# A gated scan and a top-1 mixture of experts on one Trainium2 core: the first pages picked on TensorE, loads in paced pieces, and a new order of the early work

## The chip, the core and the metric

The kernel runs on one core of one Trainium2 chip. A core has a matrix engine (TensorE, PE in the profile), a vector engine (VectorE, DVE), a scalar engine with function tables (ScalarE, ACT), a general engine (GpSimd, POOL) and a synchronisation engine that here only issues transfers (SyncE, SP). Each engine takes its instructions in the order in which the program wrote them and stands still until the semaphores of the next one are there. Transfers run on DMA engines that all queues share. The metric is the device time of one execution in microseconds (us).

## The reference

The inputs are x, r_gate and i_gate (4 sequences x 5056 steps x 256 channels, float32), a parameter per channel, and a top-1 mixture of 8 experts. The core of it:

```python
a_base = 1 / (1 + exp(-a_param))
log_a = 8 * sigmoid(r_gate) * log(clip(a_base, 1e-6, 1 - 1e-6))
a_t = exp(log_a)
x_gated = sqrt(max(1 - a_t * a_t, 1e-6)) * sigmoid(i_gate) * x
for t in range(S):                 # a scan along the steps
    h = a_t[:, t] * h + x_gated[:, t]
    y[:, t] = h
# 20224 tokens of 256 channels
logits = y @ w_gate + modality_bias[modality_id]
e_idx = argmax(logits)             # one expert a token
gate_w = softmax(logits)[e_idx]
out = gate_w * (relu(y @ w1[e_idx]) @ w2[e_idx])     # 256 -> 1024 -> 256
```

With these inputs two experts ("hot") hold nearly all tokens.

## The kernel before

**Runs and pages.** The 5056 steps are cut into runs (CHUNKS: four of 128 steps, 17 of 256, one of 128, one of 64). A run goes through: loads of a, g, x (L503, SP); tanh of both gates (L550, L535), exp (L556), square (L560) and square root (L562) on ACT; two products, the scan and a size on DVE (L541, L567, L584, L719); a scale out of that size by small matmuls (L595, L606, L608); the split of the scan's result into a high float16 part (L763, ACT) and a low one (L775, DVE); logits on PE (L789), their transpose and the routing on DVE (L845 to L913), ranks within an expert by three matmuls (L883 to L886). The routing's end is `di`, the slot of each token in a table of rows in DRAM, and `b`, how many tokens the hot experts hold by now. The split parts are turned into token rows by transposing DMAs (L814), and POOL scatters the rows to DRAM by their slots (L936).

The mixture of experts works on pages of 256 tokens of one expert (128 in the first pair). DVE chooses a pair of pages, one for each hot expert (`sel`, L1040), by a bound on what the routed runs surely hold: `choose_pages` wants the tokens of the routed runs, less `2 * behind(tokens)`, to reach those already chosen plus a pair. SP reads `sel` into a register, loads the page transposed (`X`, L1169) and its indices and gates (`mt`, L1170). PE multiplies by w1 (`ph`, L1248), ACT and DVE evacuate to a high and a low half of `H` (L1189, L1191), PE multiplies by w2 (`po`, L1290), ACT scales (`ot`, L1200) and POOL scatters to the output (L1204).

**Weights.** The four matrices of the two hot experts (w0 to w3; w2 is the first matrix of the second hot expert) are loaded (L417), measured (L340, L347) and split into a high half (HI: ACT L394 or DVE L397) and a low half (LO: "P" for PE, two passes of L382 and one of L383 with an evacuation by ACT L385; "D" for DVE, L377).

**What sets the order.** Nothing is scheduled on the chip. While the program is written, threads (Python generators) ask for an engine, with an assumed duration and a condition; `run()` takes the thread that can start first, and among those that could start within a small window after it (WINDOW, or URGENT for the early runs) the one with the lowest rank. The rank of a run's threads is a base plus C_STEP times its number. The order in which threads are taken is the order of each engine's instructions. START says in which order runs and weights ("w") are loaded at first.

```python
near = [th for th in threads if th.req[0] == eng and th.start <= first.start + th.window]
th = min(near, key=lambda th: (th.prio[eng != "PE"], th.start))
```

Of the kernel before, what the change touches and what calls it, by code (L numbers as in the profile page):

```python
# [17 lines left out]
P = 128  # L18
# [11 lines left out]
CHUNKS = [(128*k, 128) for k in range(4)] + [(512 + 256 * k, 256) for k in range(17)] + [(4864, 128), (4992, 64)]  # L30
# [6 lines left out]
WINDOW = 0.1  # L37
# [42 lines left out]
def kernel(  # L80
# [74 lines left out]
    nc.vector.tensor_scalar_add(ch, ch, 1.0)  # L155
    nc.vector.reciprocal(ch, ch)
    nc.vector.tensor_scalar(out=ch, in0=ch, scalar1=1e-6, scalar2=1.0 - 1e-6, op0=ALU.max, op1=ALU.min)

    def decay():

        yield "ACT", 0.2, seen(("tanh", 0, "a"), ("tanh", 0, "g")), None, "L"
        nc.scalar.activation(ch, ch, AF.Ln)
        table[0] = "E"
        yield "DVE", 0.1, None
        nc.vector.tensor_scalar_mul(ch, ch, 4.0)
        mark["ch"] = plan["end"] + 0.2
# [254 lines left out]
    def hot_weights(m):  # L421
# [65 lines left out]
    def load_chunk(c):  # L487
# [10 lines left out]
        for i, (name, src) in enumerate((("a", rs), ("g", gs), ("x", xs))):  # L498
            tag = "H" if c == 0 and name != "g" else name
            yield "DMA", 2.9 * z, room(tag), -9.0  # L500
            tickets[c, name] = tag, take(tag)
            t = (pm if tag == "H" else pa).tile([P, cols], F32, name=f"{name}{c}", tag=tag, bufs=BUFS[tag])
            LOADS.dma_start(t, src[:, base : base + cols])  # L503
            got.append(t)
            mark["load", c, name] = plan["end"]
# [262 lines left out]
    def low_parts(c, yg, ys, sc):  # L768
# [30 lines left out]
    def rows_part(c, j):  # L799
# [6 lines left out]
        for s in range(2):  # L806
            for h in range(2):
                yield "DMA", 0.24 * k, allof(room("rt"), high, before or high) if s == h == 0 else first if h == 0 else None, -9.0, 1.18
                if s == h == 0:
# [26 lines left out]
        mark["put", c, j] = plan["end"] + 3.0  # L836

    def route_chunk(c):
# [63 lines left out]
        with nc.allow_low_precision(reason="one whole number and zeros"):  # L902
            nc.vector.tensor_reduce(out=di, in_=ce(dt), axis=AX.X, op=ALU.add)
# [491 lines left out]
```

## Time and profile before

| what | value |
|---|---|
| median of 3 runs | 972.79 us (971.25 to 974.68) |
| the profiled execution, its own time | 970.82 us |
| its span in the profile | 969.0 us |
| mean granted clock of TensorE | 0.984 |
| busy: PE, DVE, ACT, POOL | 913.2, 667.2, 581.9, 433.4 us |
| first matmul of a page | 48.16 us |
| start of the fifth pair of pages (pair 4) | 155.02 us |

The span is cut by the profile's views in several ways: busy time of every engine in chosen stretches, a timeline of each engine in which runs of like instructions make one row (start, length, engine, line, operation, names, shapes, and in brackets the idle time before it with what ended it), and groups by line and shape. "Granted clock" is TensorE's clock as the throttle allowed it, 1.00 being full speed. Pairs of pages are counted from 0; a run's number counts from 0 too.

### The profile page before, as it was taken

To read this page: it belongs to the slowest core of one execution; us is meant where nothing else is said; L and a number is where in the kernel's file an instruction comes from. 1 tells how busy PE (TensorE), PEld (TensorE's weight loads), DVE (VectorE), ACT (ScalarE), POOL (GpSimd) and SP (SyncE) were. 2 spreads that over 40 slices of the span, in tenths; PEclk is the share of its full clock that TensorE was granted. 3 is DMA by queue.
4 is the path that set the end of the run, shared out by engine and by line. 5 is a ranking of instruction groups with operands and counts; after the bars stand their busy time and mean duration, and the time that the engine had idled before them with its cause. 6 is when DMAs were issued, how large, how long until landed. Compare 5 with 4: busy or idle time off the path is not lost. (4 is left out here: it accounts for less than half of the span.)

```text
span 969.0 us, 22431 instructions
## 1 busy us (share of the span) xinstructions
PE 913.2 (94%) x8516; PEld 789.8 (82%) x8516; DVE 667.2 (69%) x1654; ACT 581.9 (60%) x822; POOL 433.4 (45%) x539
## 2 busy tenths in 40 slices
PE   2969896999999999999999999999999999999996
PEld 2457785878888788878888888888989888888886
DVE  6887987999998989989988899743623332223321
ACT  7896766868678767688687795533333333333332
POOL 5433542663557565666655566453441212112112
PEclk9989997999999999999999999999999999999999
DMA  9766776897978889888999976635422112112110
GB/s 321 193 201 208 211 231 137 224 261 213 242 180 224 235 235 226 205 202 210 220 239 263 244 162 130 125 105 147 100 78 58 45 52 59 46 51 61 45 40 18
DMA packets 221735, 156.11 MB, mean 161 GB/s; under 512 B 198129, under 2 KB 201330, under 8 KB 215090
## 3 DMA queue, kind: packets, MB, share of 16 engines
q1 hardware_dynamic: 205296, 110.61, 48.6%
q0 software_dynamic: 16176, 43.98, 13.2%
q8 instruction: 68, 1.11, 0.5%
q14 instruction: 49, 0.40, 0.2%
q10 hardware_dynamic: 146, 0.00, 0.0%
HBM read 68.76 MB, written 44.35 MB: 117 GB/s over the span
## 5 line engine op out<-in xcount | busy, mean ns | idle before, releaser
L1248 PE MATMUL ph<-X,hw 128*128 128x256 f16 (+1 forms) x3936 | 478.4, 273 | 10.9 <-DMA X<-rows 10.9
L1290 PE MATMUL po<-hw,H 128*128 128x256 f16 x3840 | 470.9, 273 | 0.4 <-DVE H L1191 0.4
L1248 PEld LDWEIGHTS <-hw 128*128 128x128 f16 x3936 | 379.1, 99 | 59.8 <-issue 7.5
L1290 PEld LDWEIGHTS <-H 128*128 128x128 f16 x3864 | 374.6, 98 | 46.3 <-issue 1.7
L1191 DVE SCALAR_TENSOR_TENSOR H<-ph,H 128x512 f16<-128x512 f32 (+1 forms) x332 | 220.5, 668 | 240.4 <-ACT H L1189 239.6
L1189 ACT ACTIVATE H<-ph 128x512 f16<-128x512 f32 (+1 forms) x332 | 191.5, 580 | 268.7 <-PE ph L1248 266.6
L1204 POOL DMA_INDIRECT out_dram<-ot,mt x161 | 178.1, 1106 | 285.7 <-ACT ot L1200 237.7
L936 POOL DMA_INDIRECT rows<-rt,di x158 | 186.8, 1182 | 210.8 <-PE po L1290 56.7
L1200 ACT ACTIVATE ot<-po,gt 128x256 f32<-128x256 f32 x161 | 75.9, 472 | 76.8 <-PE po L1290 74.7
L584 DVE TENSOR_TENSOR_SCAN g<-a,g 128x512 f32<-128x512 f32 (+1 forms) x78 | 94.5, 1225 | 0.8
L775 DVE SCALAR_TENSOR_TENSOR a<-g,scy,a 128x512 f16<-128x512 f32 (+2 forms) x92 | 58.9, 677 | 2.9 <-ACT a L763 2.7
L763 ACT ACTIVATE a<-g,scy 128x512 f16<-128x512 f32 (+2 forms) x92 | 55.7, 654 | 0.6 <-DVE scy L615 0.6
L567 DVE SCALAR_TENSOR_TENSOR g<-x,g 128x1024 f32<-128x1024 f32 (+1 forms) x40 | 48.0, 1199 | 9.5 <-ACT x L562 9.4
L556 ACT ACTIVATE a<-a,ch 128x1024 f32<-128x1024 f32 (+2 forms) x46 | 50.7, 1115 | 0.1
L541 DVE SCALAR_TENSOR_TENSOR g<-g,x 128x1024 f32<-128x1024 f32 (+1 forms) x40 | 48.6, 1218 | 0.0
L550 ACT ACTIVATE a<-a 128x2048 f32<-128x2048 f32 (+2 forms) x23 | 38.3, 1667 | 14.7 <-DMA a<-in_r_gate_dram 14.6
L719 DVE TENSOR_REDUCE top<-x 128x4 f32<-128x2048 f32 (+2 forms) x23 | 45.4, 1974 | 2.3 <-DMA x<-in_x_dram 2.2
L562 ACT ACTIVATE x<-x,quarter 128x2048 f32<-128x2048 f32 (+2 forms) x23 | 40.5, 1761 | 0.3
L560 ACT ACTIVATE x<-a 128x2048 f32<-128x2048 f32 (+2 forms) x23 | 38.3, 1666 | 2.8 <-DVE g L541 2.5
L535 ACT ACTIVATE g<-g 128x2048 f32<-128x2048 f32 (+2 forms) x23 | 38.3, 1664 | 0.0
L562 ACT ACT_TABLE_LOAD x22 | 28.2, 1283 | 0.5
L936 POOL DMA_INDIRECT rows<-nt,ni x16 | 16.0, 997 | 19.8 <-PE po L1290 10.3
(195 smaller groups left out, 460.2 us busy)
## 6 DMA issues: line engine op xcount, KB each, us to landing
a<-in_r_gate_dram SPq DMA_DIRECT2D x17, 1024.0 KB
g<-in_i_gate_dram SPq DMA_DIRECT2D x17, 1024.0 KB
x<-in_x_dram SPq DMA_DIRECT2D x17, 1024.0 KB
wr<-in_moe_w_dram SPq DMA_DIRECT2D x4, 1024.0 KB
out_dram<-ot,mt POOLq DMA_INDIRECT x161
a<-in_r_gate_dram SPq DMA_DIRECT2D x5, 512.0 KB
g<-in_i_gate_dram SPq DMA_DIRECT2D x5, 512.0 KB
x<-in_x_dram SPq DMA_DIRECT2D x5, 512.0 KB
```

Of the source, the lines that this page charges most:

```text
L556: nc.scalar.activation(sl, sl, AF.Exp, scale=ch[:, h : h + 1], bias=ch[:, h : h + 1])
L562: nc.scalar.activation(s, s, AF.Sqrt, scale=-0.25, bias=quarter)
L584: nc.vector.tensor_tensor_scan(out=gi, data0=ai, data1=gi, initial=0.0, op0=ALU.mult, op1=ALU.add)
L763: nc.scalar.activation(ys[:, 0, :, g], yg[:, :, g, :].rearrange("p h (k b) -> p h k b", b=Q), AF.Copy, scale=sc[:, g : g + 1])
L775: nc.vector.scalar_tensor_tensor(out=ys[:, 1, :, g], in0=yg[:, :, g, :].rearrange("p h (k b) -> p h k b", b=Q), scalar=sc[:, g : g + 1], i ...
L936: ins = nc.gpsimd.indirect_dma_start(out=rows[:, :], out_offset=bass.IndirectOffsetOnAxis(ap=idx, axis=0), in_=src, in_offset=None, bounds ...
L1189: nc.scalar.activation(t.H[:, 0, hs, :], ph[:, :, 0:st], AF.Relu)
L1191: nc.vector.scalar_tensor_tensor(out=t.H[:, 1, hs, :], in0=ph[:, :, 0:st], scalar=0.0, in1=t.H[:, 0, hs, :], op0=ALU.max, op1=ALU.subtract,)
L1200: nc.scalar.activation(t.ot[:, a, :], po, AF.Copy, scale=t.gt[:, a : a + 1])
L1204: ins = nc.gpsimd.indirect_dma_start(out=out[:, :], out_offset=bass.IndirectOffsetOnAxis(ap=t.mt[:, a, 0:1], axis=0), in_=t.ot[:, a, :], i ...
L1248: ins = nc.tensor.matmul(ph[:, v, 0:st], lhsT, rhs, start=(m == 0), stop=(m == len(mm) - 1))
L1290: ins = nc.tensor.matmul(po, lhsT, rhs, start=(f == 0 and m == 0), stop=(f == NF - 1 and m == len(mm) - 1))
```

## The change

**Runs.** The first run has 96 steps instead of 128 and the last 96 instead of 64; all runs between start 32 steps earlier. **Decay.** The parameter's log (add, reciprocal, clip, Ln, times 4) is issued ahead of the first run's tanh; cpar is alone on ACT's queue, the modality bias goes to SP's. **Loads.** Run 1 is loaded ahead of the first weights (START). A load is cut into pieces of at most 128 steps (512 KB), and from run 2 on each piece waits until the piece two before it has landed. **First pages.** The first pair of pages, 128 tokens for each hot expert, isn't loaded from DRAM: DVE compares the slots of run 0 with the slots of the two pages (one-hot matrices, `pick`), and PE multiplies the token rows of run 0 by them, which gives `Xfirst` already transposed; ACT and DVE copy it out. Its `mt` is loaded as before. **Weights.** The low half of w2 is made on DVE instead of PE; of the high halves of w2 one moves from DVE to ACT. **Order.** The windows shrink, the rank of each of a run's threads gets a table (RANK), and assumed durations change. The gates of a page and the modality's bias of a run are threads of their own.

```diff
-CHUNKS = [(128*k, 128) for k in range(4)] + [(512 + 256 * k, 256) for k in range(17)] + [(4864, 128), (4992, 64)]
+CHUNKS = (
+    [(0, 96)] + [(96 + 128 * k, 128) for k in range(3)] + [(480 + 256 * k, 256) for k in range(17)]
+    + [(4832, 128), (4960, 96)]
+)
-WINDOW = 0.1
+WINDOW = 0.0
-HI = ["A", "D", "AD", "D", "A", "D"]
-LO = "PPPPDD"
-START = "0 w 1 w w w 2"
+HI = ["A", "AD", "AD", "D", "A", "D"]
+LO = "PPDPDD"
+START = "0 1 w w w w 2"
+PACED = 2
-EARLY = 8
-URGENT = 0.3
+EARLY = 7
+URGENT = 0.03
+RANK = {
+    "load": [2.5, 3.1, 0.5, 0.0, 0.0, -0.5, -2.2, 0.0, 1.4],
...
+def place(kind, c):
+    return BASE[kind] + C_STEP * c + (RANK[kind][c] if c < len(RANK[kind]) else 0.0)
...
+    nc.vector.tensor_scalar_add(ch, ch, 1.0)
+    nc.vector.reciprocal(ch, ch)
+    nc.vector.tensor_scalar(out=ch, in0=ch, scalar1=1e-6, scalar2=1.0 - 1e-6, op0=ALU.max, op1=ALU.min)
+    nc.scalar.activation(ch, ch, AF.Ln)
...
-    def decay():
-        yield "ACT", 0.2, seen(("tanh", 0, "a"), ("tanh", 0, "g")), None, "L"
-        nc.scalar.activation(ch, ch, AF.Ln)
...
+        n = max(1, T // P)
+        for name, src in (("a", rs), ("g", gs), ("x", xs)):
...
+            for i in range(n):
...
+                ins = LOADS.dma_start(t[:, i * w : (i + 1) * w], src[:, base + i * w : base + (i + 1) * w])
+                if c >= PACED:
+                    tc.add_manual_dep(
+                        ins.ins, pace[-2], mybir.DependencyInfo(mybir.DependencyClass.Sync, mybir.DependencyReason.DATA)
+                    )
+                pace.append(ins.ins.name)
...
+    def first_pages():
...
+        nc.tensor.matmul(pb[:, 0:HOT], onesf[0:1], u, start=True, stop=True)
...
+            nc.vector.tensor_scalar(out=slot[:, r], in0=along, scalar1=base[:, r : r + 1], scalar2=None, op0=ALU.add)
...
+            nc.vector.tensor_scalar(out=oh, in0=slot, scalar1=tiles["df"][:, k : k + 1], scalar2=None, op0=ALU.is_equal)
...
+                    nc.tensor.matmul(
+                        ps[:, h], tiles["rh"][:, k, s * D + h * P : s * D + (h + 1) * P],
+                        hot[k].rearrange("p r w -> p (r w)"), start=(k == 0), stop=(k == C - 1),
+                    )
...
+        if s:
+            nc.vector.tensor_copy(X[:, 2:4], ps)
+        else:
+            nc.scalar.activation(X[:, 0:2], ps, AF.Copy)
...
+                if n < HOT:
+                    t = firsts[n]
...
+                issued = [] if n < HOT else [nc.sync.dma_start_transpose(t.X, rows16[src, 0 : 2 * D])]
```

**What the order shows.** First ACT's queue at the program's start: `ch` is the decay, a, g and x are the first run's tiles; L116, L550, L535, L162, L556, L560, L562 of before are L143, L588, L573, L170, L594, L598, L600 of the change. Before:

```order
L116 ACT_TABLE_LOAD
L116 ACTIVATE ch<-cpar 128x2
L550 ACTIVATE a_241<-a_241 128x1024
L535 ACTIVATE g_243<-g_243 128x1024
L162 ACT_TABLE_LOAD
L162 ACTIVATE ch<-ch 128x2
L556 ACT_TABLE_LOAD
L556 ACTIVATE a_241<-a_241,ch 128x512 x2
L560 ACTIVATE x_245<-a_241 128x1024
L562 ACT_TABLE_LOAD
L562 ACTIVATE x_245<-x_245,quarter 128x1024
```

The change:

```order
L143 ACT_TABLE_LOAD
L143 ACTIVATE ch<-cpar 128x2
L170 ACT_TABLE_LOAD
L170 ACTIVATE ch<-ch 128x2
L588 ACT_TABLE_LOAD
L588 ACTIVATE a_247<-a_247 128x768
L573 ACTIVATE g_249<-g_249 128x768
L594 ACTIVATE a_247<-a_247,ch 128x384 x2
L598 ACTIVATE x_251<-a_247 128x768
L600 ACT_TABLE_LOAD
L600 ACTIVATE x_251<-x_251,quarter 128x768
```

The log and its table stand ahead of the first tanh, and no table load is left between the tanhs and the exps.

Then DVE around the choices (`sel`) of pairs 4 and 5, whose lines are L1040 before and L1146 in the change. Before, pair 4's and, ten rows on, pair 5's:

```order
L775 SCALAR_TENSOR_TENSOR a_1263<-g_1328,scy_1908,a_1263 128x16x32 x2
L1036 TENSOR_TENSOR d_2314<-b_2071,u 1x2
L1038 TENSOR_SCALAR d_2314<-d_2314 1x2
L1040 SCALAR_TENSOR_TENSOR sel_2313<-u,d_2314 1x2
L1044 SCALAR_TENSOR_TENSOR u<-d_2314,u 1x2
L775 SCALAR_TENSOR_TENSOR a_1263<-g_1328,scy_1908,a_1263 128x16x32 x2
L611 TENSOR_SCALAR miy_2342<-psz_2292 128x5
L615 SCALAR_TENSOR_TENSOR scy_2293<-miy_2342,s_201 128x4
L620 TENSOR_SCALAR ivy_2294<-miy_2342 128x1
L747 TENSOR_TENSOR ivl_2363<-ivy_2294,ivg 128x1
L719 TENSOR_REDUCE top_2365<-x_2227 128x4
L1036 TENSOR_TENSOR d_2398<-b_2071,u 1x2
```

The change, the choice of pair 5 (`b_2453` is what run 5 left; `H_2519` is the second page of pair 4):

```order
L1304 SCALAR_TENSOR_TENSOR H_2519<-ph_1_2559,H_2519 128x512
L622 SCALAR_TENSOR_TENSOR g_1935<-a_1711,g_1935 128x512
L1142 TENSOR_TENSOR d_2654<-b_2453,u 1x2
L622 SCALAR_TENSOR_TENSOR g_1935<-a_1711,g_1935 128x512
L1304 SCALAR_TENSOR_TENSOR H_2519<-ph_2_2600,H_2519 128x512
L1144 TENSOR_SCALAR d_2654<-d_2654 1x2
L1304 SCALAR_TENSOR_TENSOR H_2519<-ph_3_2637,H_2519 128x512
L1315 TENSOR_SCALAR gt_2698<-mt_2400,hiv_230 128x2
L1146 SCALAR_TENSOR_TENSOR sel_2653<-u,d_2654 1x2
```

Before, both pairs are chosen out of run 4's count (`b_2071`), one right after the other; in the change pair 5's choice reads run 5's and stands behind the evacuations of pair 4.

Last SP's queue where run 4 is loaded and the first page of pair 1 follows; L503, L1158, L1169, L1170 of before are L537, L1267, L1280, L1281. Before:

```order
L503 DMA a_885<-in_r_gate_dram 128x2048
L503 DMA g_981<-in_i_gate_dram 128x2048
L503 DMA x_1042<-in_x_dram 128x2048
L1158 TENSOR_LOAD sel_1061
L1158 ISA x2
L1169 ISA
L1169 DMA_TRANSPOSE X_1076<-rows 128x4x256
```

The change:

```order
L537 DMA a_915<-in_r_gate_dram 128x1024 x2
L537 DMA g_952<-in_i_gate_dram 128x1024 x2
L537 DMA x_989<-in_x_dram 128x1024 x2
L1267 TENSOR_LOAD sel_1030
L1267 ISA x2
L1280 ISA
L1280 DMA_TRANSPOSE X_1086<-rows 128x4x256
```

Three transfers of 1 MB have become six of 512 KB at the same place; the last four can be issued only as earlier ones land.

More of the change, by code (lines that the diff above doesn't have):

```diff
@@ L154, with hot_parts @@
     nc.vector.tensor_copy(order, key[:, :, 0])
[L155 to L166 removed]
+    nc.vector.tensor_scalar_mul(ch, ch, 4.0)
+    def hot_parts():
         yield "DVE", 0.1, None
@@ L234 @@
     FAR = 1e9
-    mark = {}
+    mark = {"ch": 5.0}
     slots = {t: Slots(n) for t, n in BUFS.items()}
-    free = {"PE": 0.0, "ACT": 5.2, "DVE": 7.5, "POOL": 9.0, "DMA": 1.0, "queue": 1.0}
+    free = {"PE": 0.0, "ACT": 5.7, "DVE": 5.9, "POOL": 9.0, "DMA": 1.4, "queue": 1.0}
     threads, held, table = [], [], ["E"]
@@ L479 @@
     LOADS = nc.sync
+    pace = []
     used = []
@@ L835, in rows_part @@
         give("rt", tr)
-        mark["put", c, j] = plan["end"] + 3.0
+        mark["put", c, j] = free["DMA"] + 1.2
     def route_chunk(c):
@@ L901, in route_chunk @@
         di = sm.tile([P, C], I32, name=f"di{c}", tag="di", bufs=6)
-        with nc.allow_low_precision(reason="one whole number and zeros"):
-            nc.vector.tensor_reduce(out=di, in_=ce(dt), axis=AX.X, op=ALU.add)
+        if c == 0:
+            df = tiles["df"] = sm.tile([P, C], F32, name="df", tag="df", bufs=1)
+            nc.vector.tensor_reduce(out=df, in_=ce(dt), axis=AX.X, op=ALU.add)
+            mark["slots"] = plan["end"] + 0.2
+            yield "DVE", 0.1, None
+            nc.vector.tensor_copy(di, df)
+        else:
+            with nc.allow_low_precision(reason="one whole number and zeros"):
+                nc.vector.tensor_reduce(out=di, in_=ce(dt), axis=AX.X, op=ALU.add)
         tiles["route", c] = di
@@ new lines, in first_half @@
+    def first_half(X, ps, s, tp, tx):
+        yield "DVE" if s else "ACT", 0.5, None
+        if s:
+            nc.vector.tensor_copy(X[:, 2:4], ps)
+        else:
+            nc.scalar.activation(X[:, 0:2], ps, AF.Copy)
+        give("ph", tp)
+        mark["first", s] = plan["end"] + 0.2
+        if ("first", 1 - s) not in mark:
+            return
+        for r in range(HOT):
+            t = Tile()
+            t.pg = Page()
+            t.pg.size, t.pg.st, t.pg.e = P, P, r
+            t.n, t.tx, t.X, t.mt = f"{r}", tx if r == HOT - 1 else None, X[:, :, r * P : (r + 1) * P], None
+            t.ready, t.known = plan["end"] + 0.2, FAR
+            firsts.append(t)
+            queue.append(t)
+        add(expert_layers(), (5, 0), plan["end"])
@@ L980 @@
         pass
-    pages, queue = [], []
+    pages, queue, firsts = [], [], []
     count = {"chosen": 0, "ended": False, "cold": 0, "rows": 0}
@@ L1031, in choose_two @@
         sel, ticket = new_sel()
-        b2 = tiles["b2", routed(plan["end"]) - 1]
+        b2 = tiles["b2", routed(plan["end"]) - 1 if pages else 0]
         z = size / 256
```

150 lines of the change are left out of this document (105 added, 45 removed).

## The prediction

> **What bounds the kernel now.** I read the table of busy time by stretch first (columns: stretch, length, then busy us and count of PE, PEld, DVE, ACT and POOL, granted clock, share of DMA time, GB/s).
>
> ```profile
> 0.00:10.00 10.00, 0.27 (x1) 0.18 (x2) 4.55 (x18) 4.93 (x7) 7.86 (x86) 1.00 0.79 267
> 10.00:20.00 10.00, 3.52 (x26) 2.65 (x25) 7.78 (x24) 9.84 (x12) 2.86 (x3) 1.00 1.02 359
> ...
> 60.00:70.00 10.00, 2.73 (x23) 1.47 (x22) 9.21 (x26) 9.88 (x11) 4.19 (x6) 0.73 0.78 249
> 70.00:80.00 10.00, 10.00 (x75) 8.04 (x73) 5.52 (x15) 3.10 (x6) 0.00 (x0) 0.76 0.50 82
> ...
> 100.00:150.00 50.00, 43.11 (x389) 36.51 (x388) 43.14 (x100) 36.43 (x46) 28.02 (x23) 0.96 0.71 212
> 150.00:161.00 11.00, 6.95 (x41) 4.73 (x39) 6.39 (x17) 5.82 (x5) 2.08 (x6) 0.54 0.78 123
> 161.00:500.00 339.00, 329.61 (x3124) 286.72 (x3122) 311.98 (x721) 256.95 (x327) 195.11 (x193) 0.99 0.88 223
> 500.00:962.00 462.00, 461.64 (x4387) 410.75 (x4384) 226.98 (x573) 201.13 (x332) 163.97 (x171) 1.00 0.41 99
> 962.00:969.00 7.00, 0.00 (x0) 0.00 (x0) 0.00 (x0) 0.20 (x1) 0.98 (x1) 0.76 0.04 10
> ```
>
> From 161 us on PE is the bound: 791.25 of 801 us busy. What follows its last matmul is 7 us of output. So the end is set by how early PE gets into that unbroken stretch, and by what it loses in it. The timeline of PE shows how it gets there.
>
> ```profile
> 48.16 0.83 PE L1248 MATMUL ph<-X,hw 128*128 128x128 f16 x12
> ...
> 64.70 2.09 PE L789 MATMUL psl<-a,wg 128*32 128x128 f16 x16 [4.54 <-ACT a L763]
> 69.00 6.24 PE L1248 MATMUL ph<-X,hw 128*128 128x256 f16 x30 [2.22 <-DMA X<-rows]
> ...
> 96.48 2.78 PE L1248 MATMUL ph<-X,hw 128*128 128x256 f16 x24 [2.27 <-DMA X<-rows]
> ...
> 121.76 7.08 PE L1248 MATMUL ph<-X,hw 128*128 128x256 f16 x48 [3.09 <-DMA X<-rows]
> ...
> 155.02 9.17 PE L1248 MATMUL ph<-X,hw 128*128 128x256 f16 x60 [3.29 <-DMA X<-rows]
> ...
> 165.42 1.47 PE L1248 MATMUL ph<-X,hw 128*128 128x256 f16 x12
> 166.73 1.47 PE L1290 MATMUL po<-hw,H 128*128 128x256 f16 x12
> ```
>
> These are the first pages of pairs 0 to 4; each later pair waits for its X. Twelve matmuls start 1.31 us after the twelve before them, 0.109 us each. A page of 256 tokens has 48 matmuls in each layer, so it takes 10.5 us and a pair 21. After 155.02 no matmul waits for X again. So **the event that counts is the start of pair 4**; an earlier page 0, 1, 2 or 3 only lets PE wait longer, unless pair 4 moves with it. X comes out of a chain: DVE writes the choice (sel), SP reads it, the transposed load runs.
>
> ```profile
> 149.44 0.15 DVE L1040 SCALAR_TENSOR_TENSOR sel<-u,d 1x2 int32<-1x2 f32 x1
> ```
>
> From choice to first matmul is 155.02 − 149.44 = 5.6 us. DVE issues in a fixed order, so the choice comes after the work ahead of it plus DVE's idle time. The whole stretch 0 to 150 has 121.9 us of DVE work (the sum of its busy column, with the slices not shown: 8.04, 8.84, 8.82, 8.37, 8.74, 8.85) and 28.1 us idle. The largest idle parts are 5.45 + 2.22 in the first 20 us, 4.48 in 70 to 80 and 6.86 in 100 to 150; the other seven slices hold 9.1.
>
> **The change part by part.**
>
> *Start.* The first tanh waits for cpar, and three table loads follow before the first square root.
>
> ```profile
> 6.31 0.20 ACT L116 ACTIVATE ch<-cpar 128x2 f32<-128x2 f32 x1 [3.28 <-DMA cpar<-in_a_param_dram]
> 6.42 1.04 ACT L550 ACTIVATE a<-a 128x1024 f32<-128x1024 f32 x1
> 7.36 1.04 ACT L535 ACTIVATE g<-g 128x1024 f32<-128x1024 f32 x1
> 8.42 1.28 ACT L162 ACT_TABLE_LOAD   x1
> 9.72 0.20 ACT L162 ACTIVATE ch<-ch 128x2 f32<-128x2 f32 x1
> 9.94 1.28 ACT L556 ACT_TABLE_LOAD   x1
> 11.23 1.52 ACT L556 ACTIVATE a<-a,ch 128x512 f32<-128x512 f32 x2
> 12.79 1.06 ACT L560 ACTIVATE x<-a 128x1024 f32<-128x1024 f32 x1
> 13.92 1.28 ACT L562 ACT_TABLE_LOAD   x1
> 15.21 1.15 ACT L562 ACTIVATE x<-x,quarter 128x1024 f32<-128x1024 f32 x1
> ```
>
> With cpar first on its queue, exp, Ln and two more tables end at about 3.03 + 0.2 + 1.28 + 0.2 + 1.28 = 6.0, while the first run's loads are under way; its tanh can start at 6.0 to 6.4. In the new order the exps follow the tanhs with no table between. With 96 of 128 steps the five kinds of ACT work take three quarters of 1.04, 1.04, 1.52, 1.06 and 1.15: 4.4, and one table 1.28: square root done at about 12.0, against 16.36. **Gain 4.3 us** at DVE's first long wait (it has no more to do in between). If cpar still lands at 6.31, the tables come behind it and 2.8 of that is lost.
>
> *First pages.* 12 picks of 256 columns cost PE 12 × 0.109 = 1.3 us; the two transposed loads of pair 0 leave SP, and its rows' trip through DRAM leaves the path. Four conversions (two passes, L382, one L383) and four evacuations move off PE and ACT, and four L377 come to DVE.
>
> ```profile
> 37.58 1.02 PE L382 MATMUL pl<-wr,dg 128*128 128x512 f32 x2
> ...
> 38.65 1.02 PE L382 MATMUL pl<-wr,dg 128*128 128x512 f32 x2
> ```
>
> The groups of one operation and shape (busy us, mean ns of one | idle before):
>
> ```profile
> L385 ACT ACTIVATE hw<-pl 128x512 f16<-128x512 f32 x16 | 9.4, 600 | 1.8 <-PE psl L886 0.9 <-PE pl L383 0.8
> ...
> L584 DVE TENSOR_TENSOR_SCAN g<-a,g 128x512 f32<-128x512 f32 x77 | 92.2, 1211 | 0.7
> ...
> L541 DVE SCALAR_TENSOR_TENSOR g<-g,x 128x1024 f32<-128x1024 f32 x39 | 47.8, 1231 | 0.0
> ...
> L377 DVE SCALAR_TENSOR_TENSOR cw<-cr,csc,cw 128x512 f16<-128x512 f32 x8 | 5.7, 750 | 1.0 <-ACT cw L394 1.0
> ...
> L397 DVE TENSOR_SCALAR hw<-wr,sc 128x1024 f16<-128x1024 f32 x5 | 3.8, 771 | 0.0
> ```
>
> PE saves 4 × 1.07 = 4.3 us ahead of page 0 and pays 1.3: page 0 at about 45 instead of 48.2. That by itself is worth nothing at the end, since pair 1 still waits for its own X. ACT saves 4 × 0.60 = 2.4 us, DVE pays 4 × 0.75 = 3.0.
>
> *Work ahead of the choice of pair 4.* DVE: + 3.0 (low parts), − 0.8 (one half fewer, L397), + 0.7 for half of Xfirst (as large as the H rows of 0.69 below), + 1.1 for two slots and three picks of 256 columns (an estimate, 0.2 to 0.3 each by the same row), − 2.0 for the smaller first run (a quarter of some 8 us: 1.2 for each of two products, 1.2 for each half of the scan, the rest size and split): **+ 2.0**. This stands in the new order ahead of the choice together with the same runs as before, since pairs 1 to 4 need runs 1 to 4 in both.
>
> *Idle ahead of it.* This is the term that is chosen, not read. The 4.3 of the start go. The 4.48 in 70 to 80 come from this: pair 1 starts after two PE waits of 4.54 and 2.22 us with 2 us of logits between, runs at a granted clock of 0.76, and DVE waits for its H.
>
> ```profile
> 72.41 0.69 DVE L1191 SCALAR_TENSOR_TENSOR H<-ph,H 128x512 f16<-128x512 f32 x1 [1.35 <-ACT H L1189]
> 74.97 0.69 DVE L1191 SCALAR_TENSOR_TENSOR H<-ph,H 128x512 f16<-128x512 f32 x1 [1.87 <-ACT H L1189]
> ```
>
> With X of pair 1 some 7 us earlier (4.3 and less work on ACT) and pair 0 ending about 58, the hole shrinks to 2 to 4 us: 3.5 go. In 100 to 150 the order puts the logits of run 4 inside pair 2, where before they stood behind it: 5 of 6.86. Of the other 9.1 I take 2. Sum 14.8, taken as **15**. Bounds: 4.3 alone at the low end (all else waits as before), 22.7 at the high end (all but the 5.45 of the first 10 us). The value lies nearer the high end because the three holes have rows that name their cause. Choice of pair 4: 149.4 + 2.0 − 15 = 136.4, start 142.0, **13.0 us earlier**.
>
> *Half clock.* The 60 matmuls at 155.02 take 9.17 us; at the pace of the rows behind them they take 4 × 1.31 + 1.47 = 6.7. The clock was 0.54 in that stretch. If the wait ahead of pair 4 shortens enough, these **2.5 us** go too. [...]
>
> *Run ranks and 96-step end runs.* A pair is chosen when the tokens of the routed runs, less 2 × (1.2 √tokens + 8), reach those chosen plus 512. For pair 5 that is 2,304 + 512 = 2,816. Runs 0 to 4 gave 3,072 − 149 = 2,923 before and give 2,944 − 146 = 2,798 now, so pair 5 needs run 5. Run 5's slots (di) were written here:
>
> ```profile
> 166.08 0.27 DVE L903 TENSOR_REDUCE di<-dt 128x8 int32<-128x64 f32 x1
> ```
>
> That is early enough if it shifts with the rest; the new order puts the choice behind the H evacuations of pair 4, so its X comes 0 to 2 us after PE is through with pair 4 (21 us). I take **+ 1.5**, bounds 0 and 5. The last run is 96 steps instead of 64: it lies in the stretch 500 to 962 where DVE is busy 227 of 462 us, so it costs nothing.
>
> *Paced loads.* A run of 256 steps becomes six pieces of 512 KB, at most two in flight, and SP, which is in order, stands at each.
>
> ```profile
> 104.47 0.36 SPq L503 DMA_DIRECT2D a<-in_r_gate_dram  x1
> ...
> 109.37 1.91 ACT L550 ACTIVATE a<-a 128x2048 f32<-128x2048 f32 x1 [1.66 <-DMA a<-in_r_gate_dram]
> ```
>
> 1 MB takes up to 4.9 us from issue to use. At the best rate of the table, 359 GB/s, half a MB takes 1.5 us, so what stands behind six pieces waits 4 × 1.5 = 5.8 us at SP instead of sharing the engines. I cost it at **nothing**: X is there before PE wants it all through 161 to 962. If that cover is gone, it is 5.8 us a place. [...]
>
> *Sum* against the profiled execution: 969.0 − 13.0 − 2.5 + 1.5 = **955.0** span. Its own time was 970.82 (1.8 more), and the median of the runs, 972.79, lies 2.0 above that: 955.0 + 1.8 + 2.0 = 958.8, I say **958.5 us**.
>
> **The rivals.** *A, the idle goes nearly whole* (22.7 in place of 15): 7.7 less, 951; without the wait at pair 5, 949. For it: all long waits before 150 hang on the chain X. Against: ACT is busy 9.84 and 9.88 of 10 us in 10 to 20 and 60 to 70, so DVE's waits there have a second cause. *B, pair 5 takes the place of pair 4*: run 5 is late. Run 5's di stays near 166.1, X follows at 166.1 + 0.6 + 5.6 = 172, PE would be through with pair 4 at 163: a wait of 9.3 and again 2.5 of half clock, in place of 1.5: 958.5 + 10.3 = 969. For it: one run more is wanted, and DVE is busy 312 of 339 us. Against: run 5 shares the shift of run 4. *C, slower: pieces hold X loads on SP.* Where six pieces stand ahead of an X and the lead of choices over PE is under a page (10.5 us), each place costs 5.8 + 2.5 = 8.3 us. One of them leaves 967; from the second on the gain is gone; with pairs 4, 5 and 6 all hit, 958.5 + 24.9 = 983. For it: SP issues in order, and the DMA engines are busy 0.88 of 161 to 500. Against: no row after 155.02 waits for X. *D, only the start is gained* (idle cut 4.3 and no more): start of pair 4 2.3 earlier, half clock stays: 958.5 + 10.7 + 2.5 = 972, no change; the pages picked on TensorE then do what they say and it is worth nothing.
>
> **How the numbers follow.** Forecast, with its bounds 952 to 965: 0.58. A: 0.14. B: 0.12. C: 0.09. D: 0.07. The range leaves out the far parts of A and C: 945 to 971. About 0.3%, 2.9 us, is what a measurement of this kernel tells from no change (its runs lie 3.4 apart). Faster by more than that, under 970: the forecast, A and two thirds of B, 0.81; within: the rest of B, D and a bit of C, 0.10; slower: C's rest, 0.09.
>
> **What would show it.** First square root done by 12 to 13 us; page 0 near 45; pair 1 near 62; pair 4 by 139 to 145 with PE's clock near 1 in its first 5 us; after it at most one wait for X, under 3 us, at pair 5; the PE work after pair 4's start as long as before (155 to 962, less the 2.5). I am wrong in the main step if pair 4 starts later than 150, or if it starts at 142 and the end does not follow, which B or C would show as waits for X after it.

## The result: half a per cent faster, about a third of the forecast

| | before | changed | ratio |
|---|---|---|---|
| median, 18 runs each | 973.35 us (969.80 to 977.38) | 968.25 us (961.12 to 974.24) | 0.995, 95% interval 0.9928 to 0.9971 |
| profiled execution, its own time | 970.82 us | 970.96 us | |
| its span | 969.0 us | 969.2 us | |
| first matmul of a page | 48.16 us | 45.74 us | |
| start of pair 4 | 155.02 us | 143.38 us | |

The gain is 5.1 us where 14.3 were forecast: same sign, inside the range, but far too small. One execution in all those below, of the kernel paced in runs 2 to 7 alone, took 2284 us; its ratio leaves that one out. The two profiled executions end at the same time, so the profile must show where 11.6 us at pair 4 were given back. The table of busy time by stretch of the changed kernel, with the columns as before (PE, PEld, DVE, ACT, POOL, clock, DMA share, GB/s):

```profile
60.00:70.00 10.00, 7.98 (x69) 5.57 (x70) 9.31 (x25) 9.58 (x15) 2.15 (x3) 0.83 0.81 199
70.00:80.00 10.00, 10.00 (x96) 8.97 (x95) 8.95 (x31) 9.71 (x11) 0.01 (x1) 1.00 0.66 160
...
150.00:161.00 11.00, 11.00 (x103) 9.86 (x102) 10.72 (x22) 10.98 (x14) 8.85 (x9) 1.00 0.91 277
161.00:500.00 339.00, 319.50 (x2999) 275.92 (x2998) 287.62 (x678) 246.62 (x313) 179.15 (x181) 0.98 0.89 210
500.00:962.00 462.00, 461.71 (x4387) 410.77 (x4384) 227.38 (x584) 201.71 (x332) 164.75 (x176) 1.00 0.43 106
```

In these stretches up to 161 us the table is what the prediction asked for: DVE has 8.95 instead of 5.52 in 70 to 80, and PE works through 150 to 161 at full clock. Then PE is busy 319.50 of 339, where it was busy 329.61: 10 us lost in the stretch that the prediction took to be covered. PE's timeline shows the first of them.

```profile
66.93 2.79 PE L1371 MATMUL ph<-X,hw 128*128 128x256 f16 x24 [1.02 <-DMA X<-rows]
...
93.71 6.53 PE L1371 MATMUL ph<-X,hw 128*128 128x256 f16 x36 [4.00 <-DMA X<-rows]
...
143.38 5.40 PE L1371 MATMUL ph<-X,hw 128*128 128x256 f16 x48
...
171.90 2.74 PE L1371 MATMUL ph<-X,hw 128*128 128x256 f16 x12 [5.89 <-DMA X<-rows]
...
174.77 6.61 PE L1371 MATMUL ph<-X,hw 128*128 128x256 f16 x48
```

Pair 4 starts at 143.38 without a wait. Pair 5 waits 5.89 us for X, and its first 60 matmuls then take 2.74 + 6.61 us, where the kernel without waits (e1 below) takes 1.49 + 5.41: 2.5 us of half clock. X of pair 5 had been chosen before. DVE wrote the choice at 160.26, and this is what SP did meanwhile:

```profile
160.26 0.30 DVE L1146 SCALAR_TENSOR_TENSOR sel<-u,d 1x2 int32<-1x2 f32 x1
```

```profile
146.38 3.65 SPq L537 DMA_DIRECT2D g<-in_i_gate_dram  x2
151.29 4.29 SPq L537 DMA_DIRECT2D x<-in_x_dram  x2
157.34 4.42 SPq L537 DMA_DIRECT2D a<-in_r_gate_dram  x2
164.49 2.18 SPq L537 DMA_DIRECT2D g<-in_i_gate_dram  x2
167.60 1.41 SPq L1280 DMA_TRANSPOSE X<-rows  x1
```

Eight pieces of runs 7 and 8 (g and x, then a and g) stand ahead of X, each waiting for the piece two before it. SP got from the first to the last in 20 us, about 2.5 us a piece, and issued X 7.3 us after its choice. That is rival C of the prediction at one place. Whether it is the cause, and of how much, the runs below had to tell.

### The profile page after: what moved, and what is told of

It reads as the page before. It is cut to its first block, busy times and chain, and to the rows that moved or that the text cites. A ratio compares the mean times of both kernels' runs of the same rounds, so it can differ in the third digit from the quotient of the medians.

```text
span 969.2 us, 22535 instructions
## 1 busy us (share of the span) xinstructions
PE 909.6 (94%) x8518; PEld 787.4 (81%) x8518; DVE 650.7 (67%) x1665; ACT 578.6 (60%) x819; POOL 427.8 (44%) x550
## 5 line engine op out<-in xcount | busy, mean ns | idle before, releaser
L1371 PE MATMUL ph<-X,hw 128*128 128x256 f16 (+1 forms) x3840 | 469.3, 273 | 14.8 <-DMA X<-rows 14.1
L1043 POOL DMA_INDIRECT rows<-rt,di x158 | 178.2, 1128 | 225.5 <-PE ph L1371 86.8
L594 ACT ACTIVATE a<-a,ch 128x1024 f32<-128x1024 f32 (+2 forms) x46 | 50.9, 1118 | 0.1
L588 ACT ACTIVATE a<-a 128x2048 f32<-128x2048 f32 (+2 forms) x23 | 38.4, 1671 | 20.2 <-DMA a<-in_r_gate_dram 20.1
L573 ACT ACTIVATE g<-g 128x2048 f32<-128x2048 f32 (+2 forms) x23 | 38.4, 1668 | 13.1 <-DMA g<-in_i_gate_dram 13.0
L598 ACT ACTIVATE x<-a 128x2048 f32<-128x2048 f32 (+2 forms) x23 | 38.4, 1669 | 11.2 <-DVE g L579 7.1
L600 ACT ACTIVATE x<-x,quarter 128x2048 f32<-128x2048 f32 (+2 forms) x23 | 40.6, 1763 | 0.3
```

The source lines that it names most:

```text
L594: nc.scalar.activation(sl, sl, AF.Exp, scale=ch[:, h : h + 1], bias=ch[:, h : h + 1])
L600: nc.scalar.activation(s, s, AF.Sqrt, scale=-0.25, bias=quarter)
L1043: ins = nc.gpsimd.indirect_dma_start(out=rows[:, :], out_offset=bass.IndirectOffsetOnAxis(ap=idx, axis=0), in_=src, in_offset=None, bounds ...
L1371: ins = nc.tensor.matmul(ph[:, v, 0:st], lhsT, rhs, start=(m == 0), stop=(m == len(mm) - 1))
```

## The experiments

The expectations of the first and of the paced runs number the runs at this place one too low: the pieces ahead of pair 5's X are those of runs 7 and 8, not of 6 and 7.

Three theories stood: **H**, the paced pieces hold X and later loads on SP; **L**, pair 5 needs one run more and that run is late; **C**, without pacing the loads would crowd out X and the scatters. Ratios are to the kernel before, measured beside each run, with a 95% interval. The median of the kernel before was between 970.22 and 977.92 us from one round of measurements to the next, so ratios are what is compared, and a time in us worked out from a ratio takes 970 us as its base.

### 1. Without the waits (e1)

```diff
-PACED = 2
+PACED = 99
```

> The changed kernel without the waits between pieces of a load (same pieces, same order on every engine). Its profile showed X of pair 5 chosen at 160.26 us and issued only at 167.60, behind four pieces of run 7's loads, and PE waiting 5.89 for it. Theory H (pieces hold X on SP): the 5.89 falls below 1.5, the half clock behind it (2.5) goes too, ACT's 20 us of waits for a and 13 for g shrink by half or more; time 958 to 961. Theory L (pair 5 simply needs run 5, whose choice stands too late on DVE): the wait of pair 5 stays at 4 or more, time 966 to 970. Theory C (without pacing the loads crowd out X and the scatters): X takes longer from issue to use, other waits for X appear, time 970 or more.

Measured: **952.8 us, ratio 0.9805 (0.9774 to 0.9837)**. PE, DVE, ACT and SP have the same instructions in the same order; only the waits are gone. PE and SP at pair 5, by the timeline:

```profile
166.27 1.49 PE L1371 MATMUL ph<-X,hw 128*128 128x256 f16 x12 [1.82 <-DMA X<-rows]
167.84 5.41 PE L1371 MATMUL ph<-X,hw 128*128 128x256 f16 x48
```

```profile
146.72 0.95 SPq L537 DMA_DIRECT2D a<-in_r_gate_dram  x2
148.10 0.88 SPq L537 DMA_DIRECT2D g<-in_i_gate_dram  x2
162.63 1.28 SPq L1280 DMA_TRANSPOSE X<-rows  x1
```

The same eight pieces are issued by 149, X 4.0 us after its choice (158.65), the wait is 1.82 and there is no half clock. H holds in the main: the hold and the half clock go, though the wait stays a little above the 1.5 that H named. L falls, as the choice still reads run 5 and stands where it stood. C falls: nothing is crowded out. The gain is larger than H said, 14.5 in the ratio's thousandths, some 14 us, in place of 7 to 10 us. The table of stretches tells where the rest is. First the changed kernel, then the one without waits:

```profile
0.00:143.00 143.00, 111.10 (x980) 85.40 (x981) 122.10 (x377) 112.21 (x155) 71.59 (x183) 0.96 0.80 217
143.00:180.00 37.00, 30.42 (x263) 25.18 (x262) 25.24 (x57) 28.88 (x34) 18.96 (x17) 0.91 0.87 227
180.00:250.00 70.00, 66.16 (x626) 57.19 (x624) 58.97 (x136) 52.78 (x68) 32.74 (x34) 1.00 0.93 226
250.00:500.00 250.00, 240.24 (x2271) 208.91 (x2270) 216.99 (x515) 182.67 (x234) 138.76 (x140) 0.99 0.88 206
```

```profile
0.00:143.00 143.00, 112.80 (x994) 86.67 (x995) 122.31 (x381) 113.53 (x157) 70.90 (x183) 0.96 0.78 218
143.00:180.00 37.00, 34.50 (x326) 29.94 (x325) 31.37 (x71) 33.31 (x39) 20.15 (x18) 1.00 0.90 239
180.00:250.00 70.00, 68.15 (x633) 58.91 (x631) 62.44 (x138) 53.08 (x66) 37.58 (x38) 0.98 0.86 240
250.00:500.00 250.00, 247.87 (x2366) 215.77 (x2364) 222.50 (x532) 186.97 (x243) 145.93 (x150) 1.00 0.88 216
```

PE's busy time differs by 1.7 up to 143, by 4.1 in 143 to 180 (and 2.5 of half clock there), by 2.0 in 180 to 250 and by 7.6 in 250 to 500: 17.9 of the 18.2 us between these two spans. So in these two executions **less than half of the price, 6.6 us, is at pair 5; most of the rest is small waits later**. In 250 to 500 PE waits for DVE's size and scale (mxy, dmy; the longest is 2.62 us), none of them for X. What comes late there is the run's load; ACT's waits for it in this stretch, paced and then unpaced:

```profile
ACT g L573 <- DMA g<-in_i_gate_dram: 9.9, 4, 3.6
ACT a L588 <- DMA a<-in_r_gate_dram: 5.8, 4, 2.2
```

```profile
ACT g L573 <- DMA g<-in_i_gate_dram: 5.3, 4, 1.8
ACT a L588 <- DMA a<-in_r_gate_dram: 3.8, 3, 1.6
```

15.7 us against 9.1. That these late loads are what holds PE later is read from the traces side by side, not shown by a run of its own. That these waits belong to the pacing is better founded: in the same stretch PE is busy 246.97, 244.93, 246.48 and 246.08 us in e2, e3, e13 and e14 below, where nothing is paced or four pieces may be in flight.

### 2 and 3. Whole loads (e2), and four pieces in flight (e3)

```diff
-                w = cols // n
-                ins = LOADS.dma_start(t[:, i * w : (i + 1) * w], src[:, base + i * w : base + (i + 1) * w])
...
+                if i == 0:
+                    LOADS.dma_start(t, src[:, base : base + cols])
```

> The changed kernel with whole loads as before (1 MB at once, no pieces, no waits; the order of every engine but SP is the same). Theory H: the same as without the waits, 958 to 961, within 2 of it, since the number of pieces by itself costs nothing. If pieces by themselves cost, this one is 3 or more faster than the pieces without waits. Theory L: 966 to 970. Theory C: 970 or more, as before's loads crowd the start.

Measured: 954.31 us, ratio 0.9819 (0.9787 to 0.985).

```diff
-                        ins.ins, pace[-2], ...
+                        ins.ins, pace[-4], ...
```

> The changed kernel, where a piece waits for the piece four before it (2 MB in flight instead of 1). Theory H: most of the hold on SP goes, the wait of pair 5 falls to 1 to 3, time 960 to 964, between the paced and the unpaced one. Theory L: no change, 966 to 970. Theory C: slower than 969.

Measured: 953.7 us, ratio 0.9824 (0.9792 to 0.9856). The three intervals overlap: cutting a load into pieces costs and gives nothing that can be measured, and with 2 MB in flight the pacing is as good as gone. What cost was the depth of two. H had put both kernels at 958 to 964 us, so here too it held the price for smaller than it was.

### 4. The kernel before, with nothing but paced pieces (e4)

```diff
...
+                if c >= 2:
+                    tc.add_manual_dep(
+                        ins.ins, pace[-2], ...
...
+                pace.append(ins.ins.name)
```

> The kernel before with nothing but its loads cut into paced pieces (each waits for the piece two before it, from run 2 on; the order of the other engines is unchanged). Theory H: X loads and later loads stand behind the pieces, one or more new waits of 3 to 6 us, time 976 to 984. Theory L: no difference, 971 to 975. Theory C: faster, 965 to 971, as X loads get the DMA engines for themselves.

Measured: **980.09 us, ratio 1.0088 (1.0055 to 1.0122)**. Pacing alone makes the kernel before slower by 9 us, so it has a price without the rest of the change, too: 8.8 thousandths, against 14.5 with it. H holds for the time and C falls here too; but H's new waits for X don't show. PE waits for X nowhere behind pair 4, and the longest new wait, 3.7 us, is for a size (mxy). Pair 4 of this kernel starts at 158.24 instead of 155.02, and PE is busy 324.57 of 339 in 161 to 500 instead of 329.61:

```profile
158.24 8.82 PE L1258 MATMUL ph<-X,hw 128*128 128x256 f16 x60 [3.15 <-DMA X<-rows]
...
212.92 1.91 PE L1300 MATMUL po<-hw,H 128*128 128x256 f16 x12 [2.39 <-ACT ot L1210]
217.30 0.27 PE L605 MATMUL psz<-identb,mxy 128*4 128x128 bf16 x1 [2.48 <-DVE mxy L743]
```

### 5 and 6. Paced from run 8 on (e5), and runs 2 to 7 only (e6)

```diff
-PACED = 2
+PACED = 8
```

> The changed kernel, paced only from run 8 on (runs 2 to 7 unpaced, whose pieces held X of pair 5). Without any pacing the ratio to before was 0.9805, with all of it 0.995: pacing costs about 14 us. Theory P5 (the hold at pair 5, 5.9 and 2.5 of half clock, is most of the price): ratio 0.985 to 0.988, 957 to 960. Theory T (runs that land late later on, ACT waiting 33 us for a and g in place of 17, are most of the price): 0.990 to 0.994, 963 to 967.

Measured: 957.78 us, ratio 0.9845 (0.9818 to 0.9873).

```diff
-                if c >= PACED:
+                if PACED <= c < 8:
```

> The other half: only runs 2 to 7 are paced. Theory P5: X of pair 5 held 4 to 6 us, half clock behind it, ratio 0.989 to 0.991, 961 to 964. Theory T: 0.982 to 0.985, 954 to 957. If the two prices add up, this one and the one paced from run 8 on lie together 14 above the kernel without pacing.

Measured: 960.01 us, ratio 0.9857 (0.9825 to 0.989). The first half lies 4.0 and the second 5.2 thousandths above the kernel without waits, both together 14.5. The first comes out at the edge of P5's range, the second between T's and P5's. The intervals are about 3 thousandths each way, so the ratios alone don't show that the two prices fail to add up; the profiles show why they need not. In both kernels one of runs 7 and 8 is unpaced, and in both X of pair 5 leaves SP no later after its choice than without any waits (4.0), 3.5 and 4.2 us (choices at 162.00 and 163.76). The rows of pair 5, first e5, then e6:

```profile
170.52 2.74 PE L1371 MATMUL ph<-X,hw 128*128 128x256 f16 x12 [2.72 <-DMA X<-rows]
```

```profile
171.57 2.68 PE L1371 MATMUL ph<-X,hw 128*128 128x256 f16 x12 [2.00 <-DMA X<-rows]
```

So in these executions **the hold needs both runs paced**, nine pieces in a row (the eight and one of run 7's a ahead of them); that is why neither half shows it. The 12 matmuls behind the wait still run at half clock in both, which with the matmuls behind them costs 1.3 and 1.5 us.

What else each half costs, these two profiles can't say. The first wait of e5 stands in run 8, whose first piece left SP at 156.07, yet its pair 4 had started at 144.78, 2.95 us later than in e1; so much can part two executions ahead of any wait. DVE's first two halves of H in pair 3, one for every twelve matmuls, start 2.56 us apart there (123.09 and 125.65), where twelve matmuls start 1.31 us after the twelve before them in pair 4; that pair 3 had fallen into half clock is an estimate from these two numbers. And in 250 to 500 PE is busy 245.57 us in e5 and 245.59 in e6, where no load is paced any more: both lie among the kernels without effective waits (244.93 to 247.87) and far from 240.24 with all paced.

### 7. All paced but runs 6 and 7 (e15)

```diff
-                if c >= PACED:
+                if c >= PACED and c not in (6, 7):
```

> The changed kernel, paced but for runs 6 and 7, whose pieces are those that stand ahead of pair 5's X on SP. Theory P5 (the hold at this place: 5.9, less 1.8 that stays without pacing, and 2.5 of half clock): 6 to 7 faster than all paced, ratio 0.988 to 0.989. Theory T (late loads all through): 0.992 to 0.995. If the holds pass to another place: no gain, with a new wait for X of 3 or more behind 170 us.

Measured: 964.32 us in a round in which the kernel before took 977.92, ratio 0.9861 (0.9832 to 0.989), 8.9 thousandths better than all paced. Of the two runs ahead of pair 5's X this frees run 7, and the hold and the half clock go:

```profile
167.16 0.14 DVE L1146 SCALAR_TENSOR_TENSOR sel<-u,d 1x2 int32<-1x2 f32 x1
```

```profile
168.78 1.20 SPq L1280 DMA_TRANSPOSE X<-rows  x1
```

```profile
174.04 1.48 PE L1371 MATMUL ph<-X,hw 128*128 128x256 f16 x12 [2.06 <-DMA X<-rows]
```

X leaves 1.6 us after its choice instead of 7.3. In this execution pair 4 came late, at 148.40, so the place is measured from there: pair 5 starts 25.64 us after pair 4, against 28.52 with all paced and 24.44 in e1. With the half clock, 2.5, that is 5.4 us won back of the 6.6 that the hold cost. In 250 to 500 PE is busy 244.99 us, so freeing two runs helped the later ones too, and the two can't be parted by this run. Theory T alone (0.992 to 0.995) falls; P5's range lies inside the interval.

### 8 to 13. Parts of the change undone, the rules free to order anew (e7 to e12)

All of these are without the waits, so they stand against 0.9805.

```diff
# e7
-    add(first_pages(), (0, PICK_AT), urgent=True)
...
-                issued = [] if n < HOT else [nc.sync.dma_start_transpose(t.X, rows16[src, 0 : 2 * D])]
+                issued = [] if n < 0 else [nc.sync.dma_start_transpose(t.X, rows16[src, 0 : 2 * D])]
# e8
-WINDOW = 0.0
+WINDOW = 0.1
-C_STEP = 2.89
+C_STEP = 2
-EARLY = 7
-URGENT = 0.03
+EARLY = 8
+URGENT = 0.3
-    return BASE[kind] + C_STEP * c + (RANK[kind][c] if c < len(RANK[kind]) else 0.0)
+    return BASE[kind] + C_STEP * c 
# e9
-    nc.scalar.activation(ch, ch, AF.Ln)
...
+        yield "ACT", 0.2, seen(("tanh", 0, "a"), ("tanh", 0, "g")), None, "L"
+        nc.scalar.activation(ch, ch, AF.Ln); table[0] = "E"; yield "DVE", 0.1, None
# e10
-HI = ["A", "AD", "AD", "D", "A", "D"]
-LO = "PPDPDD"
+HI = ["A", "D", "AD", "D", "A", "D"]
+LO = "PPPPDD"
# e11
-CHUNKS = [(0, 96)] + ... + [(4832, 128), (4960, 96)]
+CHUNKS = [(128*k, 128) for k in range(4)] + ... + [(4864, 128), (4992, 64)]
# e12
-START = "0 1 w w w w 2"
+START = "0 w 1 w w w 2"
```

The high half that changes its engine in e10, and in the change itself, is one of w1 (the second entry of HI), not of w2; of w2 it is the low half alone (the third entry of LO).

> Unpaced, with the first pair of pages scattered to DRAM and loaded transposed as before, instead of picked on TensorE (the pick's matmuls, copies and one-hot work are gone; all else of the change stays). By the prediction's step the pages' way is worth nothing at the end, since pair 1 waits for its own X: 951 to 955, ratio 0.979 to 0.983; page 0 starts 3 to 6 later. Rival: the earlier pages free SP, DMA or buffers and pull pair 4 ahead: 957 or more.

Measured: 964.28 us, ratio 0.9914 (0.9886 to 0.9942).

> Unpaced, with the order rules as before: no rank table, C_STEP 2, windows 0.1 and 0.3, 8 early runs. Theory O (the new order is the gain: idle taken out of DVE's queue ahead of pair 4): pair 4 starts 8 or more later than 142, time 961 or more. Theory S (the start, 4.3 us, and the smaller first run, the weights and the early runs' loads carry it): 951 to 957.

Measured: 977.47 us, ratio 1.0043 (1.0026 to 1.006).

> Unpaced (953 us, 0.9805 of before), with the decay's log behind the first run's tanhs again. The prediction gave the earlier log 4.3 us together with the smaller first run; in the profile of the change the first square root ended at 14.1 in place of 16.4, so 2.3. If the start passes through to pair 4: 955 to 958, ratio 0.983 to 0.986. If the chain ahead of pair 4 absorbs it: 952 to 954, ratio 0.979 to 0.982.

Measured: 961.02 us, ratio 0.9888 (0.9865 to 0.9912).

> Unpaced, with the low parts of w2 on TensorE and its high halves on VectorE as before. By the prediction's step PE's four conversions are worth nothing at the end (page 0 some 3 us later, ACT 2.4 more, DVE 2.2 less ahead of pair 4): 950 to 955. If ACT is what sets the choice of pair 4 (it is 98% busy from 30 to 60 us), 956 or more.

Measured: 973.34 us, ratio 1.0021 (1.0004 to 1.0039).

> Unpaced, with the runs cut as before (first run 128 steps, last 64). Pair 5 is then chosen out of run 4 again: its wait of 1.8 us goes, but the first run's work is a third longer, 1.5 us on ACT and 2.0 on DVE ahead of pair 4. By the prediction's terms about level: 951 to 956. If the small first run is where the gain begins: 958 or more.

Measured: 963.3 us, ratio 0.9911 (0.9884 to 0.9938).

> Unpaced, with the first weights loaded ahead of run 1 again. Run 1's gates come 2 to 3 us later, the conversions 2 to 3 earlier. By the prediction only the choice of pair 4 counts, and it hangs on the runs: 954 to 957. If the weights' conversions set the first pages and these the rest: 949 to 952.

Measured: 975.98 us, ratio 1.004 (1.0026 to 1.0054).

By their times e7, e10 and e11 would fall to the second reading of each, e8 to theory O, and e9 and e12 to neither. But undone one by one, the six parts cost 8 to 23 us each (by the ratios), far more together than the 18.9 that all of them gave. No sum of parts can be right here. The choice of pair 4 shows what happened, in two of the three kernels with the largest loss (e10, then e12; 133.93 in e1, with no part undone):

```profile
160.91 0.15 DVE L1146 SCALAR_TENSOR_TENSOR sel<-u,d 1x2 int32<-1x2 f32 x1
```

```profile
153.25 0.15 DVE L1146 SCALAR_TENSOR_TENSOR sel<-u,d 1x2 int32<-1x2 f32 x1
```

and PE behind them:

```profile
166.16 5.28 PE L1371 MATMUL ph<-X,hw 128*128 128x256 f16 x24 [5.28 <-DMA X<-rows]
```

```profile
157.48 5.20 PE L1371 MATMUL ph<-X,hw 128*128 128x256 f16 x24 [11.70 <-DMA X<-rows]
```

Four conversions more on PE are 4 us of work (1.07 each by the prediction's rows), yet the choice of pair 4 moved by 27. With another part in place the rules had taken threads in another order, and DVE's queue had other work ahead of that choice: 377 and 372 instructions in place of 350, which keep it busy for 128.97 and 128.43 us in place of 115.12, and it stands idle for 31.9 and 24.8 in place of 18.8. With the pages loaded from DRAM (e7), pairs 2 and 3 even started earlier than in e1 (85.1 and 111.2 us against 92.0 and 118.7) and pair 4 later (149.2 against 141.8); the end followed pair 4 (a span of 961.8 us against 951.0).

### 14 and 15. Two parts undone with the order held (e13, e14)

The log was put behind the first tanhs, and the first weights' load ahead of run 1's, with every other instruction of PE, DVE, ACT and SP where it stood.

```diff
# e13
-    nc.scalar.activation(ch, ch, AF.Ln)
-    nc.vector.tensor_scalar_mul(ch, ch, 4.0)
...
+    def late_log(c):
+        if c == 0 and ("tanh", 0, "a") in mark and ("tanh", 0, "g") in mark:
+            nc.scalar.activation(ch, ch, AF.Ln); nc.vector.tensor_scalar_mul(ch, ch, 4.0)
...
# e14
+                if c == 1:
+                    waiting.append((t, src[:, base : base + cols])); continue
...
         nc.sync.dma_start(v, src)
+        while waiting:
+            nc.sync.dma_start(*waiting.pop(0))
```

> Unpaced, with the log and its tables behind the first run's tanhs, but every other instruction of every engine left where it stands (the run before it with a late decay let the rules order all the rest anew, and cost 8 us). Theory W (the part itself is worth it): the first square root ends 2 to 3 later and the end follows, 955 to 957, ratio 0.982 to 0.985. Theory O (the new order it made cost the 8): 952 to 954, ratio 0.979 to 0.982.

Measured: 956.55 us in the same round as the run before (the kernel before at 977.92), **ratio 0.9789 (0.9756 to 0.9822)**.

> Unpaced, with the first weights' load ahead of run 1's on SP's queue, and nothing else moved (with the rules free to order the rest anew it cost 23 us). The load of 1 MB delays run 1's gates by 2.4 to 3 us. Theory W: the delay passes to the choices, 955 to 957, or more if it passes several times. Theory O: 951 to 954, run 1 waits on ACT for less than what is idle there.

Measured: 954.62 us, **ratio 0.9768 (0.9736 to 0.9799)**.

Both are level with 0.9805 (0.9774 to 0.9837): at a held order neither part is worth anything that can be measured, and by the intervals not more than some 3 us. The choice of pair 4 came at 131.00 and 132.40 us, no later than e1's 133.93. With the rules free they had cost 8 and 23 us. What the free runs measured was the new order, not the part. For the other four parts this was not tried.

**The faster version** is that of the first run: all of the change without the waits between pieces, 952.8 us, by the ratios 1.95% under the kernel before and 1.5% under the change as it was made.

## Why the prediction was wrong

**The step that failed: "Paced loads … I cost it at nothing: X is there before PE wants it all through 161 to 962."** Measured: 14.5 thousandths, some 14 us, by the ratios 0.995 and 0.9805. That no matmul waited for X in the old trace was a fact of the old trace, in which SP issued a whole run's loads from 104.47 to 106.51. The change took that lead away: SP needed 2.5 us a piece, where the 5.8 of the prediction counts 1.5. Rival C had the mechanism and the price of one place (5.8 + 2.5; measured 5.89, of which 1.82 stay without pacing, and 2.5) and said "one of them leaves 967"; the median is 968.25. It had a chance of 0.09 and was read as X alone. The larger part of the price, the small waits for size and scale behind pair 5, was in no rival; that late a and g make them is argued, not shown. That C's 967 lies so near is luck: these waits, some 7.5 us, were missing from it, and so was a gain of some 4 that the kernel without waits has beyond the forecast.

**Pair 4.** Forecast 142.0; 143.38 with waits, 141.83 without. Its time came out, and the half clock at its start (2.5) went as said (48 matmuls in 5.40 us with waits and without). As an event it holds for the large step and not for each us: in the profiled executions of e1, e2, e3, e13 and e14 pair 4 starts between 138.24 and 144.34, and their spans are 950.9 to 953.6, so 6 us of start leave less than 3 at the end. And the working behind it was partly wrong, so that it came out this well is luck:

- *Start, 4.3 us.* The first square root ended at 14.06 instead of 16.36: 2.3. ACT was through with the exps at 8.4, a little before what was worked out (8.7), and then stood:

```profile
5.62 0.84 ACT L588 ACTIVATE a<-a 128x768 f32<-128x768 f32 x1
...
7.10 1.29 ACT L594 ACTIVATE a<-a,ch 128x384 f32<-128x384 f32 x2
10.91 0.84 ACT L598 ACTIVATE x<-a 128x768 f32<-128x768 f32 x1 [2.51 <-issue]
11.83 1.28 ACT L600 ACT_TABLE_LOAD   x1
13.12 0.94 ACT L600 ACTIVATE x<-x,quarter 128x768 f32<-128x768 f32 x1
```

  The square writes over x, which DVE's product has to read first, and DVE made the slots of the new first pages and the size ahead of that product, after a wait of 1.57 us for a table of theirs (`along`) from POOL:

```profile
8.12 0.99 DVE L980 TENSOR_SCALAR slot<-along,base 128x128 f32<-128x128 f32 x2 [1.57 <-POOL along L253]
9.03 0.93 DVE L760 TENSOR_REDUCE top<-x 128x4 f32<-128x768 f32 x1
9.88 0.94 DVE L579 SCALAR_TENSOR_TENSOR g<-g,x 128x768 f32<-128x768 f32 x1
```

  With the log behind the tanhs (e13) the same square root ends at 13.88. There the exps end at 10.59, no later than the product lets the square begin anyway. The order of log and tanh, which the step counted, gave nothing; what is left to explain the 2.3 is that cpar lands early (its exp starts at 2.59 instead of 6.31) and the run is smaller.
- *Work + 2.0, idle − 15.* The choice of pair 4 came at 135.47 against 136.4, but not by these terms. The stretch up to the choice, before and then changed:

```profile
0.00:149.44 149.44, 114.57 (x965) 87.47 (x966) 121.34 (x344) 117.19 (x160) 70.70 (x169) 0.95 0.74 224
0.00:135.47 135.47, 103.57 (x910) 79.07 (x911) 115.35 (x350) 109.36 (x150) 68.33 (x180) 0.96 0.80 218
```

  DVE's idle time fell from 28.10 to 20.12, by 8.0 and not by 15, and its busy time fell by 6.0 where 2.0 more were counted. The two errors cancel. The work itself did not shrink: the durations of the 344 and 350 instructions add up to 136.2 and 137.0 us. But an instruction begins before the one ahead of it has ended (in the rows above, at 9.03 under one that ends at 9.11), and the busy column counts such a stretch once; by the two sums, 14.9 us overlap before (136.2 − 121.34) and 21.7 in the change (137.0 − 115.35), where the queue is packed more densely. No term had this. Of the idle terms, the holes at 70 to 80 (4.48 to 1.05) and behind 100 (6.83 to 1.94) closed as said; the first 20 us gave 1.7 instead of 4.3; and the other slices grew by 2.0 instead of shrinking by 2, with pair 1 at 66.93 where 62 was said.

**Pair 5, + 1.5.** It came out at 1.82 without pacing, with no half clock behind it (12 matmuls in 1.49 us). Rival B, whose 969 lies nearer the measured time than the forecast, had the wrong mechanism: run 5's slots were ready at 142.85, 23 us earlier than before.

**After pair 4: "as long as before".** Wrong both ways. From pair 4's start to the span's end were 814.0 us before, 825.8 with the waits and 809.2 without; with the half clock and the wait at pair 5 the prediction's terms give 813.0. Without the waits between pieces the small waits for size and scale in 250 to 500 shrink from 7.2 us of idle PE before to 2.1; this 5 us gain, which no term had, is most of what takes 18.9 past the forecast 14.3. In e2, e3, e13 and e14 the same idle time is 3.0 to 5.1. Why it shrinks was not settled.

**First pages, "worth nothing at the end".** Page 0 came at 45.74, forecast 45. Whether the pick itself is worth something stays open: e7 cost 10.6 us, but with another order.

**Chances.** Faster had 0.81 and came, but not with the working: the step at pair 4 was mostly given back behind it, and the time lies in the range because it reaches into rival C.

## What to carry to other kernels

That nobody waits for a transfer in the old trace is a fact of the lead with which it is issued there, and a change that delays its issue spends that lead: here eight paced pieces took SP 20 us, X left 7.3 us after its choice in place of 4.0, and PE waited 5.89 us in place of 1.82. So price such a change by the time that the queue now needs to get to the last issue, for every transfer behind it, not by the waits of the old trace. And where rules order a whole program, undoing one part measures the order that the rules then make: hold the order fixed before a price is put on a part.

## What the runs showed of the hardware

- Two 512 KB loads in flight passed SP at about 2.5 us a piece in 146 to 167 us, with scatters beside them (11 by POOL; DMA share 0.86, 264 GB/s), so one was under way for an estimated 5 us (two in flight at 2.5 us a piece). The prediction's estimate from the best rate of the table was 1.5. The pieces themselves, unpaced, cost nothing that can be measured (0.9805 against 0.9819 with whole loads).
- Half clock followed a wait of 5.89 us (12 matmuls in 2.74 us, granted clock 0.50 in 171.9 to 174.7) but also waits of 2.00 and 2.72 (12 matmuls in 2.68 and 2.74 us in e6 and e5), while none followed 2.06 or 1.82 (1.48 and 1.49 in e15 and e1). So in these runs the length of the wait ahead doesn't decide between 2.00 and 2.06 us. What does decide, no run here shows.
- The changed kernel's 18 runs spread over 13.1 us, those of before over 7.6. Without the waits six runs lay within 2.8 in e1 (950.72 to 953.53), but within 7.8 in e13, so the spread is not put down to the waits.
